# Batch 0 of a gated attention and mixer kernel: 64-row mode and mirror blocks from its third block on, and one spaced list of loads

## The chip, the core and the metric

The kernel runs on one core of a Trainium2 chip. The metric is the device time of one execution in microseconds (us), as the median of several runs. The span of a profile is a little shorter than that time, since it begins with the first instruction and ends with the last.

TensorE multiplies matrices into PSUM[...]. ScalarE (ACT) and VectorE (DVE) read PSUM and write SBUF. GpSimd (POOL) and SyncE (SP) here mainly start DMA transfers: GpSimd the loads from HBM, which turn float32 into bfloat16 on the way, SyncE the transposes from SBUF to SBUF and the stores.

## What is computed

For each of 8 batches, with S = 3008 rows and D = 256 columns (z has 64 columns):

```python
scores = (z @ z.T) / S
attn = maximum(scores, 0) ** 2
x = u * (attn @ v)                          # gated attention: the mixer's input
h = maximum(x.T @ w_tok1, 0) @ w_tok2       # token mixer, 3008 -> 256 -> 3008
u2 = x + h.T
out = u2 + maximum(u2 @ w_ch1, 0) @ w_ch2   # channel mixer, 256 -> 1536 -> 256
```

The matrix of scores is symmetric. So is its relu squared: the block of rows g and columns q is the transpose of the block of rows q and columns g.

## The kernel before

**Tiles.** The 3008 columns are cut into six query blocks q of 512 (the last has 448), the rows into six groups g of four tiles of 128. A block (b, q, g) of the attention matrix is made by two *score units* of two tiles each. A unit is two matmuls of 64 rows that run side by side in TensorE's upper and lower half (z has only 64 columns), into a pair of PSUM banks. ScalarE takes the pair out with a relu (line 461), VectorE squares it in place (469), and the result lies in one of six `at` buffers. When all six g have been multiplied with v, block q is finished, gated with u into `xT`, and turned by a DMA transpose into `x_sb`.

**Mirror blocks.** `direct_block` says which blocks are scored. For batches 1 to 7 these are the ones with g >= q; the block below the diagonal is a *flip*: a DMA transpose of the whole `at` buffer (`flip`, line 514) into an `fl` buffer. An `at` buffer that is flipped comes free only when the transpose has read it. On the diagonal only the triangle is scored and its other half turned in place (`flip_tiles`, 507). In batch 0 all 36 blocks are scored and nothing is flipped. The `fl` buffers (ten) first hold batch 0's six slices of v.

**Two modes of TensorE.** *Half*: pairs of 64-row matmuls. Scores are always in this mode, and so are batches 1 to 7's attention times v (line 644): the upper and the lower 64 rows of a tile go to two banks of a pair, and at the end of a block ScalarE copies one of them out (725), VectorE adds the other (729) and gates the sum (749). *Full*: 128-row matmuls. Batch 0's attention times v runs in it (`whole_matmul`, line 561), into one bank for each half of the 256 columns, and is gated straight from there. The mixer is always full. While a block is *whole*, score units are issued in runs of up to three, to change the mode less often. Two PSUM banks are whole blocks' accumulators; when the last whole block is done they become a fourth pair for the ring of pairs that all else shares (`ring`, `take_slot`).

**The planner.** The order of instructions is decided when the kernel is built, by a loop (from line 1199) that keeps a clock of its own for TensorE, ScalarE, VectorE and SyncE with costs written in the code. At each step it picks a score unit, a piece of attention times v ("av"), or a piece of the mixer. The pieces of a batch's mixer are added when its last block ends: `tok1` (line 800), `tok2` (h_ps, 818), `ch1` (hp, 862), `ch2` (op, 906). A budget spreads them over the next batch. On the chip only semaphores hold: each engine runs its list in order and waits for what it needs.

**Loads.** Before, batch 0's loads are bound to positions in the order of attention blocks (`at_group`): z and v of batch 1, u, and then the four weights (`items`). They carry no wait but for their buffers. From batch 1 on, loads are asked for by `ask`, and `ask_some` lets one go at least `SPACING` = 4.5 us of the planner's clock after the one before. Ahead of it GpSimd copies one element of the newest squared block (`after`, line 120), so that on the chip the load starts no earlier than that.

```python
if asks and pe[0] >= last_ask[0] + SPACING and asks[0][1]():
    last_ask[0] = pe[0]
    if recent[0] is not None:
        after(recent[0])
    asks.pop(0)[0]()
```

Of the kernel before, what the change touches and what calls it, by code (L numbers as in the profile page):

```python
# [55 lines left out]
def kernel(  # L56
# [141 lines left out]
    def load_v(b, c):  # L198
        if b == 0:

            vt = sb.tile([P, GK, D], BF16, tag="fl", name="v_sb", bufs=ROOM["fl"])
            live["fl"] += 1
        else:
            vt = sb.tile([P, GK, D], BF16, tag="v", name="v_sb", bufs=8)
        n = full_tiles[c]
        nc.gpsimd.dma_start(out=vt[:, :n, :], in_=rows_of(v[b], c))
        if n < GK:
            for r in range(2):
                nc.gpsimd.dma_start(
                    out=vt[r * TAIL:(r + 1) * TAIL, n, :], in_=last_rows(v[b]))  # L210
        vs[b, c] = vt
        v_in[b, c] = Done(pe[0] + 9.0 if b > 1 else 0.0)
        loading(LOAD)

    def load_u(b, q):
# [47 lines left out]

    zTs, vs, urs, uTs, xTs, xs = {}, {}, {}, {}, {}, {}
    v_in = {}
    attn = {}

    def direct_block(b, q, g):  # L270

        return b == 0 or g >= q

    def flips(b, q, g):

# [255 lines left out]
    class Block:  # L531
        def __init__(self, b, q):
            self.b, self.q, self.W = b, q, widths[q]
            self.todo = key_order(b, q)[1]
            self.slot = 0
            self.g = None
            self.steps, self.half = [], 0
            self.acc = [None] * DT
            self.home = [None] * DT
            self.begun = set()  # L540
            self.whole = b == 0
            self.tails = False
            self.parts = {}

# [57 lines left out]
    def do_whole(start, g):  # L602
        blk = cur[0]
        begins = blk.g is None
        if begins:
            blk.g, blk.half = g, 0
            blk.todo.remove(g)
            blk.slot += 1
            blk.parts.setdefault(g, 2 if g == LAST else 1)
            n = grain(blk.b, blk.q, g)  # L610
            tiles = list(range(GK - 1 if g == LAST else GK))
            blk.steps = [(dh, tiles[i:i + n]) for i in range(0, GK, n) for dh in range(DT)]
        final = blk.slot == NG
        if begins:
            if final and not blk.tails:
                do_tails(blk, max(start, tails_ready(blk)))
                start = pe[0]
        dh, tiles = blk.steps[blk.half]
        start, end = on_pe(start, "full", len(tiles) * column_time(blk.W))
        for i in tiles:  # L620
            whole_matmul(blk, g, i, dh, final and i == tiles[-1])
        if final:
            acc_free[dh] = push(
                "dve", end + 0.21, 0.61, 0.75,
                lambda t, dh=dh: gate(blk, dh, blk.acc[dh], t), first=1,
                room=("xT", "x") if dh == 0 else lambda: (blk.b, blk.q) in xTs)
        blk.half += 1
        if blk.half == len(blk.steps):
            blk.g = None
            finished(blk, g)  # L630
            if final:
                end_block(blk)
                if blk.q == NQ - 1:
                    ring.append((acc_free[-1], RING))

    def av_matmul(blk, g, i, dh, h, stop):
# [39 lines left out]
    def do_half(start, g):  # L676
# [25 lines left out]
        if blk.half == len(blk.steps):  # L702
            blk.g = None
            _, _, name, uses = blocks.pop((blk.b, blk.q, g))
            release(name, uses, pe[0] + 0.2)
            used[blk.b, g] = used.get((blk.b, g), 0) + 1
            if final:
                end_block(blk)

# [6 lines left out]
    def finish(blk, dh, end):  # L716


        W, acc = blk.W, blk.acc[dh]
        summed = Done()  # L720
        ring.append((summed, blk.home[dh]))

        def copy(t):
            cp = sb.tile([P, QW], F32, tag="res", name="cp", bufs=3)
            nc.scalar.copy(cp[:, :W], acc[:, 1, :W])  # L725
            push("dve", t, 0.66, 0.78, lambda t: add(cp, t), first=1, done=summed)

        def add(cp, t):
            nc.vector.tensor_add(cp[:, :W], acc[:, 0, :W], cp[:, :W])  # L729
            push("dve", t, 0.58, 0.7, lambda t: gate(blk, dh, cp, t), first=1,  # L730
                 room=(lambda: (blk.b, blk.q) in uTs and has_room(("xT", "x"))) if dh == 0
                 else lambda: (blk.b, blk.q) in xTs)

        push("act", end + 0.21, 0.46, 0.61, copy, first=1)

    gated = [0]

    def gate(blk, dh, acc, t):
        b, q, W = blk.b, blk.q, blk.W
        uT = uTs[b, q]  # L740
        if dh == 0:
            xTs[b, q] = sb.tile([P, DT, QW], BF16, tag="xT", name="xT", bufs=ROOM["xT"])
            live["xT"] += 1
            live["x"] += 1
            if W < QW:
                nc.gpsimd.memset(xTs[b, q][:, :, W:], 0.0)
        xT = xTs[b, q]
# [8 lines left out]
        if dh == DT - 1:  # L756
            gated[0] += 1
            push("sp", t, 1.25, 7.5, lambda t: turn_x(b, q, t), first=1)

    def turn_x(b, q, t):  # L760
        x = sb.tile([P, DT, QW // P, P], BF16, tag="x", name="x_sb", bufs=ROOM["x"])
        nc.sync.dma_start_transpose(
            out=x.rearrange("p h t d -> p (h t) d"),
            in_=xTs[b, q].rearrange("p h s -> p (h s)"))
# [18 lines left out]
    def add_mixer(b):  # L783
# [6 lines left out]
        def tok1(q, end):  # L790
# [2 lines left out]
                st["a_ps"] = bank_pair(st["a_slot"], "a_ps")[:, 0, :].rearrange(  # L793
                    "p (h d) -> p h d", h=DT)
            x = xs.pop((b, q))
            live["x"] -= 1
            for i in range(QW // P):
                k = q * (QW // P) + i
                for th in range(2):
# [147 lines left out]
            heads.append(Piece(0.874, [x_done[b, NQ - 1]], lambda end, q=q: tok1(q, end),  # L947
                               opens=q < NQ - 1, closes=q > 0))
        for q in range(NQ):
            heads.append(Piece(4 * column_time(widths[q]), [a_done],  # L950
                               lambda end, q=q: tok2(q, end)))
        def add_ch1(q, c2):
            h2_done[q, c2] = Done()
# [113 lines left out]
    def ask(fn, ready=None):  # L1067
        asks.append((fn, ready or (lambda: True)))

    def ask_some():  # L1070


        while later and later[0][1]() and pe[0] >= later[0][0]:
            later.pop(0)[2]()
        if asks and pe[0] >= last_ask[0] + SPACING and asks[0][1]():
            last_ask[0] = pe[0]
            if recent[0] is not None:
                after(recent[0])
            asks.pop(0)[0]()

    def u_then_turn(m):
        load_u(m // NQ, m % NQ)
# [8 lines left out]
    for b in range(B):  # L1091
        base = b * NQ * NG
        for q in range(NQ):
            m = b * NQ + q + 2
            if m < B * NQ:
                if b == 0:
                    at_group(base + q * NG + 2, lambda m=m: load_u(m // NQ, m % NQ))
                    at_group(base + q * NG + 5, lambda m=m: turn_u(m // NQ, m % NQ))
                else:
# [1 line left out]
        if b + 1 < B:  # L1101
            at_group(base + NG, lambda b=b: new_zT(b + 1))
            for j, c in enumerate(vorder):
                if b == 0:
                    at_group(base + NG + j, lambda b=b, j=j: load_z(b + 1, j))
                    if j % 3 == 2:
                        at_group(base + NG + j // 3 + 8, lambda b=b, j=j: turn_next_z(b, j // 3))
                else:
                    at_group(base + 2 * NG + 2 + j,
                             lambda b=b, j=j: ask(lambda: z_then_turn(b + 1, j)))  # L1110
                    at_group(base + (NQ - 1) * NG - 2 + (j if j > 1 else 0),
                             lambda b=b, c=c, j=j: ask(
                                 lambda: load_v(b + 1, c),
                                 lambda: j < 2 or used.get((b, vorder[j - 2]), 0) == NQ))
    def late_z(c, landed):


# [36 lines left out]

    at_group(6, lambda: turn_u(0, 1))
    w_done = [Done() for _ in range(4)]

    def ask_w_ch(part):
        load_w_ch(part)
        w_done[part].t = pe[0] + 16.0  # L1160


    items = [lambda c=c: load_v(1, c) for c in vorder]
    items += [lambda c=c: load_w_tok1(c) for c in range(NG)]
    items += [lambda c=c: load_w_tok2(c) for c in range(NG)]
    items += [lambda part=part: ask_w_ch(part) for part in range(4)]
    for k, item in enumerate(items):
        at_group(NG + 1 + k * (NQ * NG - 2 * NG + 4) // len(items), item)

    per_batch = 0.87 * NQ * (2 + CHT // 2) + 1.35 * 4 * NQ  # L1170
    flat = NQ * NG * 1.73 + NQ * (NQ + 1) / 2 * 0.44
# [21 lines left out]
    STARVED = 0.7  # L1193
    BACKLOG = 0.9
    SWING = 2.0
    SPACING = 4.5
    SLOW = 0.84
    LONG = 12.0
    while cur[0] is not None or heads or tails:
        run_engines(pe[0])  # L1200
        ask_some()
# [33 lines left out]
        queued = max(free["act"], t) + sum(op.busy for op in waiting["act"]) - t  # L1235


        spare = True
        if blk is not None and not runs:
            if None in blk.acc:  # L1240
                spare = len(slots) > 1 and slots[1] <= t + NOW
            elif blk.slot == NG and blk.g is None:
                spare = len(slots) > 1
            elif blk.slot == NG and blk.half == len(blk.steps) - 1:
                spare = len(slots) > 1 and slots[1] <= t + 0.8

        between = blk is None or blk.acc[0] is None
        mixer_now = tm <= t + NOW and (budget > -SWING or blk is None)
        pick = None

        together = (
# [2 lines left out]
        if not runs:  # L1254
            if mode[0] == "full" and mixer_now:
                pick = "mixer"
            elif mode[0] == "half" and between and budget > LONG and mixer_now:
                pick = "mixer"
            elif n_now and spare and queued < BACKLOG and ts <= t + NOW:
                pick = "scores"  # L1260
            elif ta <= t + NOW:
                pick = "av"
            elif n_now and spare and ts <= t + NOW:
                pick = "scores"
            elif mixer_now:
                pick = "mixer"
# [12 lines left out]
            pick = "av"  # L1279
        if pick is None:  # L1280
            options = [(ta, "av"), (tm, "mixer")]
            if n_now and (whole or low if runs else spare):
                options.append((ts, "scores"))
            when, what = min(options)
            op = next_op()
# [58 lines left out]
```

## Time and profile before

| what | before |
|---|---|
| time, median of 3 | 1154.92 us (1154.44 to 1154.99) |
| span of the profiled execution | 1152.1 us |
| score matmuls (64 rows) | 732 |
| attention times v, 128 rows / 64 rows | 288 / 3948 |
| flips of whole blocks, median from issue to landing | 105, 4.9 us |
| last attention matmul of batch 0, about | 91 us |

Engines' busy times are sums of what the profiler shows. A matmul's shown duration contains its way through the array, so neighbours overlap: a row of "mean 376 ns" can start every 216 ns. "64*128" is a matmul on half of the rows. In the chain and the waits, "A <- B" says that A waited for B. For a DMA, "issue" is the time on the queue that starts it and "landing" is when its last byte is in place.

### The profile page before, as it was taken

The page shows a single profiled execution, that of the slowest core. Times are in us where ns is not written, and L with a number is a line of the kernel's source. Part 1 is how long each engine was busy: PE and PEld are TensorE (multiplying, and loading weights), DVE is VectorE, ACT ScalarE, POOL GpSimd, SP SyncE. Part 2 cuts the span into 40 slices and gives each one's busy share as a digit, 9 for nine tenths or more (in the row PEclk, how much of TensorE's full clock was granted, in tenths as well). Part 3 has the DMA queues.
Part 4 walks back from the last instruction along what each step waited for, and adds up shares of the span by engine and source line. Part 5 has one row for each costly group of instructions (what it writes and reads, how often), then busy time and mean ns, then how long its engine had stood idle before and what let it go on. Part 6 is the DMA issues. An engine that isn't in the chain of part 4 may idle for free.

```text
span 1152.1 us, 22026 instructions
## 1 busy us (share of the span) xinstructions
PE 1141.6 (99%) x8989; PEld 652.5 (57%) x8989; DVE 627.6 (54%) x940; ACT 552.0 (48%) x706; POOL 148.4 (13%) x387
## 2 busy tenths in 40 slices
PE   9999999999999999999999999999999999999998
PEld 3335464655556465575565655656556555566666
DVE  6666754456535664447545475453655556433544
ACT  7887633355434733437435364253463555422321
POOL 4500001110112001210011100121012110000000
PEclk9999999999999999999999999999999999999999
DMA  9998957899869959799488985789759997632121
GB/s 162 182 184 147 182 132 131 142 176 161 150 130 184 162 126 164 130 193 170 105 156 141 188 169 116 147 136 185 149 111 182 158 181 157 129 87 56 51 83 64
DMA packets 472517, 165.80 MB, mean 144 GB/s; under 512 B 436257, under 2 KB 450145, under 8 KB 472417
## 3 DMA queue, kind: packets, MB, share of 16 engines
q1 hardware_dynamic: 444560, 131.70, 56.5%
q0 software_dynamic: 27344, 32.32, 21.1%
q8 instruction: 70, 1.15, 0.4%
q10 hardware_dynamic: 512, 0.38, 0.1%
q14 instruction: 31, 0.25, 0.1%
HBM read 65.40 MB, written 24.64 MB: 78 GB/s over the span
## 4 chain that ended last, share of the span: by engine, by line
PE 95%; DMA 2%; ACT 1%; DVE 1%; SPq 0%; issue 0%; POOL 0%; ACTq 0%; DVEq 0%
PE acc L644 35%; PE op L906 21%; PE hp L862 21%; PE sc L423 6%; PE first_acc L561 5%; PE h_ps L818 3%; PE a_ps L800 3%; DMA fl<-at 1%; ACT at L461 1%; DMA zf<-in_z_dram 1%; DMA at<-at 0%; DMA v_sb<-in_v_dram 0%; SPq L510 0%; DVE h2pre L878 0%; DVE xT L749 0%
## 5 line engine op out<-in xcount | busy, mean ns | idle before, releaser
L461 ACT ACTIVATE at<-sc 128x1024 bf16<-128x1024 f32 (+1 forms) x284 | 279.6, 1021 | 96.3 <-PE sc L423 88.1
L644 PEld LDWEIGHTS <-v_sb 64*128 64x128 bf16 x3948 | 201.3, 94 | 211.1 <-issue 7.2
L876 ACT ACTIVATE h2pre<-hp 128x1024 bf16<-128x1024 f32 (+1 forms) x163 | 163.2, 1003 | 296.4 <-PE hp L862 296.3
L644 PE MATMUL acc<-at,v_sb 64*128 64x512 bf16 x2268 | 280.3, 375 | 0.2 <-DMA at<-at 0.2
L469 DVE TENSOR_TENSOR at<-at 128x1024 bf16<-128x1024 bf16 (+1 forms) x284 | 195.0, 689 | 141.1 <-ACT at L461 139.1
L862 PE MATMUL hp<-xT,w_ch_sb 128*128 128x512 bf16 (+1 forms) x1152 | 257.4, 375 | 0.0
L906 PE MATMUL op<-w_ch_sb,h2pre 128*128 128x256 bf16 x2208 | 251.4, 273 | 0.3 <-DVE h2pre L878 0.2
L906 PEld LDWEIGHTS <-h2pre 128*128 128x128 bf16 x2208 | 215.2, 98 | 39.0 <-issue 3.3
L878 DVE TENSOR_SCALAR h2pre<-hp 128x1024 bf16<-128x1024 f32 (+1 forms) x125 | 150.9, 1208 | 97.3 <-PE hp L862 96.8
L644 PE MATMUL acc<-fl,v_sb 64*128 64x512 bf16 (+1 forms) x1680 | 193.6, 367 | 0.8 <-DVE xT L827 0.7
L862 PEld LDWEIGHTS <-w_ch_sb 128*128 128x128 bf16 x1152 | 111.6, 98 | 126.1 <-issue 5.7
L919 DVE TENSOR_TENSOR res<-op,u_sb 128x512 f32<-128x512 f32 x87 | 60.2, 692 | 142.8 <-PE op L906 140.8
L423 PE MATMUL sc<-zT 64*128 64x512 bf16 (+1 forms) x732 | 124.5, 358 | 0.6 <-ACT at L461 0.3
L729 DVE TENSOR_TENSOR cp<-acc,cp 128x512 f32<-128x512 f32 (+1 forms) x84 | 56.3, 675 | 91.3 <-ACT cp L725 90.5
L725 ACT COPY cp<-acc 128x512 f32<-128x512 f32 (+1 forms) x84 | 48.7, 580 | 102.8 <-PE acc L644 102.5
L449 ACT ACTIVATE at<-sc 128x512 bf16<-128x512 f32 (+3 forms) x164 | 60.8, 438 | 39.9 <-PE sc L423 38.1
L561 PE MATMUL first_acc<-at,v_sb 128*128 128x512 bf16 (+2 forms) x288 | 65.6, 376 | 1.3 <-DMA v_sb<-in_v_dram 1.3
L423 PEld LDWEIGHTS <-zT 64*128 64x128 bf16 x732 | 37.7, 94 | 46.8 <-issue 12.6
L498 DVE TENSOR_TENSOR at<-at 128x512 bf16<-128x512 bf16 (+3 forms) x164 | 45.5, 322 | 25.4 <-ACT at L449 24.3
L827 DVE TENSOR_TENSOR xT<-xT,h_ps 128x1024 bf16<-128x1024 bf16 (+1 forms) x48 | 55.2, 1173 | 7.1 <-PE h_ps L818 6.8
L749 DVE TENSOR_TENSOR xT<-cp,uT 128x512 bf16<-128x512 f32 (+1 forms) x84 | 55.4, 665 | 0.8
L120 POOL CAST mark<-at 128x1 f32<-128x1 bf16 x48 | 10.2, 213 | 334.2 <-DVE at L469 334.2
(55 smaller groups left out, 369.0 us busy)
## 6 DMA issues: line engine op xcount, KB each, us to landing
out_dram<-res SPq DMA_DIRECT2D x87, 256.0 KB, 2.3
v_sb<-in_v_dram POOLq DMA_DIRECT2D x40, 256.0 KB, 5.7
ur<-in_u_dram POOLq DMA_DIRECT2D x40, 256.0 KB, 5.5
w_tok_sb<-in_moe_w_tok_dram POOLq DMA_DIRECT2D x10, 256.0 KB, 9.2
zs<-in_z_dram POOLq DMA_DIRECT2D x35, 64.0 KB, 3.7
at<-at SPq DMA_TRANSPOSE x123, 2.7
fl<-at SPq DMA_TRANSPOSE x105, 4.9
v_sb<-in_v_dram POOLq DMA_DIRECT2D x8, 192.0 KB, 5.7
```

The costliest lines, as they stand in the source:

```text
L423: nc.tensor.matmul(sc[:, r, c0:c1], zT[h, k:k + P], zT[h, m + c0:m + c1], start=True, stop=True)
L449: nc.scalar.activation(a3[:, i, c0:c1], sc[:, r, c0:c1], ACT.Relu, scale=inv_S)
L461: nc.scalar.activation(view, sv, ACT.Relu, scale=inv_S)
L469: nc.vector.tensor_mul(view, view, view)
L561: nc.tensor.matmul(o, vs[blk.b, g][rows, i, dh * P:(dh + 1) * P], rhs, start=first, stop=stop, skip_group_check=True)
L644: nc.tensor.matmul(o, vs[blk.b, g][rows, i, dh * P:(dh + 1) * P], rhs, start=(dh, h) not in blk.begun, stop=stop, skip_group_check=True)
L729: nc.vector.tensor_add(cp[:, :W], acc[:, 0, :W], cp[:, :W])
L862: nc.tensor.matmul(hp[:, r, :W], w_ch1_sb[:, dc, cc * P:(cc + 1) * P], xT[:, dc, :W], start=(dc == 0), stop=(dc == DT - 1))
L876: nc.scalar.activation(h2[:, :, :W], hp[:, :, :W], ACT.Relu)
L878: nc.vector.tensor_single_scalar(h2[:, :, :W], hp[:, :, :W], 0.0, AX.max)
L906: nc.tensor.matmul(op[:, i, :], h2, w_ch2_sb[:, cc, :], start=(cc == 0 and (i == 0 or apart)), stop=(cc == CHT - 1), skip_group_check=True)
L919: nc.vector.tensor_add(res.rearrange("p i (h d) -> p i h d", d=P), op.rearrange("p i (h d) -> p i h d", d=P), us[:, :, half * 2:half * 2 + ...
```

## The change

Batch 0's blocks q = 0 and 1 stay whole. From q = 2 on the batch runs in half mode, and with g >= 2 it uses the symmetry: six blocks, (3,2), (4,2), (4,3), (5,2), (5,3) and (5,4), become flips instead of scores. To leave DMA room for these flips, every load from block 1 on goes through one list, one load per 2.4 us of the planner's clock in batches 0 and 1; the weights are taken from it only when nothing else is due. As they come later, the mixer doesn't begin before batch 1's third block (`OPENING`). The copy at the end of a half block of batch 0 goes to whichever of ScalarE and VectorE is less loaded, and batch 0's `x_sb` uses the buffers of `h2`, which are idle then.

```diff
-        return b == 0 or g >= q
+        return g >= q or (b == 0 and g < MIRROR)          # WHOLE, MIRROR = 2, 2
...
-            self.whole = b == 0
+            self.whole = b == 0 and q < WHOLE
...
-                if blk.q == NQ - 1:
+                if blk.q == WHOLE - 1:
                     ring.append((acc_free[-1], RING))
...
+        on_act = blk.b > 0 or load("act") + 0.46 < load("dve") + 0.67
...
+    def x_home(b):
+        return "x" if b else "h2"
...
-            heads.append(Piece(4 * column_time(widths[q]), [a_done],
+            heads.append(Piece(4 * column_time(widths[q]), [a_done, tok2_done[q]],
...
-        if asks and pe[0] >= last_ask[0] + SPACING and asks[0][1]():
-            last_ask[0] = pe[0]
-            if recent[0] is not None:
-                after(recent[0])
-            asks.pop(0)[0]()
+        spacing = SPACING if cur[0] is None or cur[0].b > 1 else FIRST_SPACING
+        if pe[0] < last_ask[0] + spacing:
+            return
+        if asks and asks[0][1]():
+            fn = asks.pop(0)[0]
+        elif spare:
+            fn = spare.pop(0)
+        else:
+            return
+        last_ask[0] = pe[0]
+        if recent[0] is not None:
+            after(recent[0])
+        fn()
...
-    items = [lambda c=c: load_v(1, c) for c in vorder]
-    items += [lambda c=c: load_w_tok1(c) for c in range(NG)]
-    items += [lambda c=c: load_w_tok2(c) for c in range(NG)]
-    items += [lambda part=part: ask_w_ch(part) for part in range(4)]
-    for k, item in enumerate(items):
-        at_group(NG + 1 + k * (NQ * NG - 2 * NG + 4) // len(items), item)
+    weights = [lambda c=c: load_w_tok1(c) for c in range(NG)]
+    weights += [lambda c=c: ask_w_tok2(c) for c in range(NG)]
+    weights += [lambda part=part: ask_w_ch(part) for part in range(4)]
+    at_group(NG + 1, lambda: spare.extend(weights))
+    for k, c in enumerate(vorder):
+        at_group(3 * NG + k, lambda c=c: ask(lambda: load_v(1, c)))
...
-    SPACING = 4.5
+    FIRST_SPACING, SPACING = 2.4, 4.5
+    OPENING = NQ + 2
...
-        mixer_now = tm <= t + NOW and (budget > -SWING or blk is None)
+        opening = blk is not None and blk.b * NQ + blk.q < OPENING
+        mixer_now = tm <= t + NOW and (budget > -SWING or blk is None) and not opening
```

## The prediction

> **What bounds the kernel now.** I read the page's first part, the list of waits, a piece of the timeline and then the DMA views, because the answer of each raises the next question.
>
> ```profile
> PE 1141.6 (99%) x8989; PEld 652.5 (57%) x8989; DVE 627.6 (54%) x940; ACT 552.0 (48%) x706; POOL 148.4 (13%) x387
> ```
>
> TensorE is bound from end to end. So a gain has to come out of its instruction stream or out of its few holes, which the list of waits for TensorE names:
>
> ```profile
> PE a_ps L800 <- ACT at L461: 0.9, 1, 0.9
> PE h_ps L818 <- ACT at L461: 0.8, 2, 0.6
> PE acc L644 <- DVE xT L827: 0.7, 1, 0.7
> PE acc L644 <- DMA at<-at: 0.2, 1, 0.2
> ```
>
> A busy share overstates a pipelined engine, so I took starts of matmuls in the trace instead. A 128-row matmul of 512 columns starts 216 ns after the one before; two 64-row ones together take 217 ns. The timeline shows what a change between the two modes costs:
>
> ```profile
> 61.90 0.82 PE L423 MATMUL sc<-zT 64*128 64x512 bf16 x6
> 62.65 2.76 PE L561 MATMUL first_acc<-at,v_sb 128*128 128x512 bf16 x12
> 65.34 0.61 PE L423 MATMUL sc<-zT 64*128 64x512 bf16 x4
> ```
>
> From 62.65 to 65.34 is 2.69 us for twelve matmuls of 0.216, 2.59: 0.10 is the switch. With 0.095 a switch, the 8989 matmuls need 1125.5 + 114 x 0.095 = 1136.3 us. The first starts at 1.2, the last ends at 1147.7: 10.1 us are holes. By the starts, 3.8 of them lie before 20 us, 0.6 at 102 (the scores waiting for ScalarE), 2.4 between 122 and 131 (around the h_ps burst), 1.1 at 238, and the rest in crumbs.
>
> The second reading is the DMA, by stretches (last two numbers: busy share of its engines, GB/s):
>
> ```profile
> 50.00:75.00 25.00, 25.00 (x134) 9.71 (x133) 17.86 (x27) 21.27 (x23) 5.38 (x9) 1.00 1.25 189
> 100.00:125.00 25.00, 24.07 (x213) 12.92 (x208) 14.15 (x26) 17.18 (x24) 0.92 (x3) 1.00 1.06 187
> ```
>
> It is full while TensorE notices nothing, because in batch 0 nothing that TensorE needs soon comes from a transpose. From 36 to 75 us the loads take most of it:
>
> ```profile
> q0 software_dynamic: 4036, 5.35, 81.1%
> q1 hardware_dynamic: 7910, 1.94, 40.3%
> ```
>
> The zT transposes behind them took a median of 16.1 us from issue to landing. The view of the flips from 88 to 125 us, where one load at a time is under way, says:
>
> ```profile
> L517 SPq DMA_TRANSPOSE fl<-at x9: 1582/1949/5817, 90.9 to 122.2; - x9
>   ACT at L461: 1.9, 2
> DMA to landing us min/median/max: 3.9/5.8/7.9
> ```
>
> A flip holds SyncE for 1.95 us and lands 3.9 to 7.9 us after its issue; ScalarE has already waited 1.9 us for a buffer that a flip was still reading.
>
> **What the skill says.** "TensorEngine Tiling (Array Packing)", Key Properties: changing the tiling mode drains TensorE. The trace agrees, 0.10 us each. "DMA: Bandwidth & Descriptors", Issuing engines are not separate DMA queues: transfers of all engines run on the same 16 DMA engines and interleave. The trace agrees (zT 16.1 us beside loads; 2.5 to 2.8 us alone later on). The same page, Latency and other measured facts, gives 261 GB/s for DMA transposes; a flip moves 0.524 MB, so an estimate is 2.0 us, beside 1.95 measured on SyncE.
>
> **The change part by part.**
>
> *64-row mode from block (0,2) on.* The streaming time of attention times values stays (288 x 0.216 against pairs of 0.217). What goes is switching: in whole mode every run of three score units costs two. In the order of the changed program I count 86 switches for 114: 28 x 0.095 = 2.7 us off the path, as TensorE has nothing else then. It adds, for 4 blocks x 2 halves, a copy (0.48 on ScalarE or 0.60 on VectorE back to back) and an add (0.60). ScalarE: 12 units x 0.92 + 2 x 0.48 = 12.0 us in a block of 13.0 us of TensorE; hidden, barely. VectorE: 12 x 0.61 + 6 x 0.60 = 10.9; hidden.
>
> *Six mirror blocks.* (3,2), (4,2), (4,3), (5,2), (5,3), (5,4) are no longer scored: 12 units x 0.216 (four of them 0.19) and, in the counts, 732 score matmuls become 708: 72.1 to 69.7 us, so 2.4 us off. ScalarE loses 12 x 0.92, VectorE 12 x 0.61, both slack. In their place come six flips: 6 x 1.95 us of SyncE and of DMA, at 34 to 66 us.
>
> The stream is then 1123.0 + 8.2 = 1131.2 us: **5.1 us less**, if holes stay.
>
> *Spaced list, weights last.* Before, loads of batch 0 carried no wait and ran ahead. Now each follows a marker on GpSimd that waits for the newest squared block, one per about 2.9 us of TensorE's work. Behind the marker only later loads are queued; the weights, at the end, are wanted only by the mixer, which begins later. A load costs the DMA about 1.28 us (39 us x 81.1/121.4 over 20.4 loads of 0.262 MB). So DMA is 44% taken by loads, and the flips live on the rest.
>
> *Does the flips' queue keep up?* This is the unknown cost. SyncE's queue is in order. From 34 us (TensorE's work time, holes left out) to the flip of block (0,3,5), fl_798, stand four flips, two x, one u and five z transposes: 4 x 1.95 + 3 x 1.26 + 5 x 1.2 = 17.6 us, with seven loads of 1.28 between, 9.0: it is served at 60.6 and lands 2 us later, 62.6. Who wants it: block (0,4,1) was given the buffer that this flip still reads (buffers of the changed program); its score is issued at 58.2, and the PSUM bank of that score is the next acc1's at 60.2. ScalarE must begin by 59.2: 3.4 us late. With 1.0 us a load it is 1.5, with transposes at the 2.9 us of the 88-125 stretch (81% of 37 us over 5.5 MB) it is over 7. I take 2.5, as loads of one at a time leave gaps.
> Between 77 and 105 us there are 17.5 us of transposes (five flips for batch 1) and 7 loads, 9.0: the triangle of (1,1), at_1263, lands near 105.5 and is wanted at 104.6, with the first 2.5 us already giving it time: 1.0. fl_1560 at 114 and at_1447 at 129 have margins near zero: 0.5. Sum **4.0 us of new holes**, ends 0.5 and 15.
>
> *Mixer from block 8.* The pieces are the same (2256 + 1152 + 192 + 384 matmuls in both orders) and only come later. The holes of 102 and 122-131, 3.0 us, go with the old order; but the new one has five h_ps in a row with only two free PSUM pairs, each evacuated in 1.13 us by VectorE against 0.86 of TensorE: 5 x 0.27 = 1.35, plus the bank's turn-round of 0.2 twice: 1.8 back. x of batch 0 moving into h2's buffers, and the tok2 waits, cost nothing: no h2 is alive before the first ch1 at 126 us, and the last tok2 slice is asked for 15 us ahead of its use.
>
> Total: -5.1 + 4.0 - 3.0 + 1.8 = -2.3, rounded to the profile's crumbs: 1154.9 - 2.6 = **1152.3 us**.
>
> **Rivals.**
> A, *the queue falls behind*: with transposes slowed by loads as at 36-75 us, holes come to 8 to 15 us (fl_798 5 to 8, at_1263 and fl_1247 3 to 4, at_1447 2 to 3). Then 1154.9 - 5.1 - 3.0 + 1.8 + 10 = 1158.6, slower. For it: DMA at 187-189 GB/s already, 3.1 MB more flips in the same stretch, the 16.1 us of zT. Against: there the loads ran ahead in a heap; now they are spaced.
> B, *it cancels*: holes of 6 us give 1154.6.
> C, *all hidden*: the queue keeps up as after 250 us, where TensorE has crumbs only, and the h_ps burst costs nothing: 1154.9 - 5.1 - 3.0 = 1146.8 or, with the usual crumb, 1147.5.
>
> **How the numbers follow.** My forecast (holes 2 to 5): 0.35; C: 0.15; B: 0.2; A: 0.3. Faster by over 0.2% (below 1152.6) is C and most of my forecast, 0.5; same 0.2; slower 0.3. Range 1147.3 to 1160.0: C's end is in, and of A the far half is out.
>
> **What would show it.** Right: the switches' 2.7 us and the scores' 2.4 us in TensorE's starts before 110 us; a wait of ScalarE for fl<-at of 1 to 4 us near 64 us (60 + 3.9 of start holes); flips landing 4 to 15 us after their issue. Wrong: TensorE holes over 8 us between 50 and 135 us, by fl<-at or at<-at; or TensorE waiting for ScalarE in every block, which would mean that 12.0 of 13.0 us is too tight; or weights landing after tok1 (near 108 us).

## The result, and the profile after

The changed kernel takes 1171.53 us (median of 4 runs, 1170.83 to 1173.65); the kernel before took 1154.95 beside it. The ratio is 1.0147, 95% interval 1.0130 to 1.0165: 17 us slower. The forecast was 1152.3. On the chips of the experiments further down, some runs of most kernels took about 10 us longer than the rest (17 of 55 runs of the kernel before on one chip), which makes the intervals wide; a ratio leaves out runs over 1.5% above the fastest of their kernel.

First the busy row, TensorE's row in the 40 slices and the clock granted to it, from the page of the changed kernel:

```profile
PE 1143.4 (98%) x9149; PEld 662.5 (57%) x9149; DVE 625.8 (54%) x938; ACT 546.3 (47%) x700; POOL 155.2 (13%) x419
...
PE   9987899999999999999999999999999999999998
...
PEclk9998999999999999999999999999999999999999
```

TensorE's busy share hardly moved. The slices show where to look: the third to fifth (58 to 146 us). Next, TensorE's waits in the changed kernel (us in total, times, longest):

```profile
PE sc L424 <- ACT at L462: 6.2, 2, 5.9
PE acc L645 <- ACT at L462: 5.7, 1, 5.7
PE acc L645 <- DMA at<-at: 4.2, 2, 2.3
```

Two waits for ScalarE of nearly 6 us and two for the triangle (the diagonal block whose other half is turned in place) are new. ScalarE's own waits between 40 and 170 us say what it waited for:

```profile
ACT at L462 <- DMA fl<-at: 15.1, 4, 6.6
```

A flip still reads the buffer into which ScalarE is to write: the chain is TensorE, ScalarE, flip. The flips around the first long hole, between 57 and 70 us:

```profile
L518 SPq DMA_TRANSPOSE fl<-at x2: 2937/3110/3282, 61.6 to 65.0; - x2
...
  ACT at L462: 6.3, 1
...
DMA to landing us min/median/max: 5.0/5.9/6.7
```

The one that ScalarE waits for was issued at 61.6 us and landed 6.7 us later, at 68.3. The flips between 88 and 125 us, in the view that the prediction showed of before:

```profile
L518 SPq DMA_TRANSPOSE fl<-at x5: 3882/4677/6576, 87.8 to 112.3; - x5
...
  ACT at L462: 8.8, 3
...
DMA to landing us min/median/max: 7.3/9.5/12.3
```

The median flip held SyncE 1.95 us before and 4.7 now; it landed 5.8 us after its issue before and 9.5 now. The table of stretches, two of the kernel before and then the changed kernel's (TensorE's busy time comes second, the last three numbers are granted clock, DMA share and GB/s):

```profile
125.00:150.00 25.00, 23.98 (x173) 12.20 (x171) 19.74 (x30) 14.06 (x20) 3.23 (x8) 1.00 0.95 178
150.00:175.00 25.00, 25.00 (x185) 17.65 (x184) 10.99 (x12) 6.14 (x6) 1.42 (x4) 1.00 0.48 116
```

```profile
50.00:75.00 25.00, 18.79 (x162) 9.19 (x160) 14.41 (x23) 14.01 (x16) 6.06 (x14) 0.93 1.02 179
75.00:100.00 25.00, 25.00 (x248) 13.20 (x245) 19.25 (x35) 20.38 (x26) 8.07 (x21) 1.00 1.11 179
100.00:125.00 25.00, 18.76 (x148) 8.93 (x146) 9.03 (x16) 9.50 (x14) 6.93 (x16) 0.86 1.22 178
125.00:150.00 25.00, 20.79 (x158) 10.45 (x155) 8.74 (x12) 7.69 (x9) 4.68 (x12) 0.93 1.19 191
150.00:175.00 25.00, 23.01 (x163) 10.26 (x162) 17.52 (x28) 16.04 (x23) 4.71 (x12) 1.00 1.17 187
```

Two things are to be seen. The DMA's share is over 1 from 50 to 175 us; before, it was 0.95 at 125 to 150 and 0.48 at 150 to 175. That alone stops nothing: at 50 to 75 us the share is lower than before (1.02, before 1.25), and only now does somebody wait there for a flip. And the clock is no longer 1.00: a mean of 0.86 in 25 us is 7 us at half clock, 0.93 is 3.5. TensorE's timeline shows how the two hang together:

```profile
61.94 1.91 PE L645 MATMUL acc<-at,v_sb 64*128 64x512 bf16 x16
69.50 1.89 PE L645 MATMUL acc<-at,v_sb 64*128 64x512 bf16 x8 [5.65 <-ACT at L462]
...
103.89 1.04 PE L645 MATMUL acc<-at,v_sb 64*128 64x512 bf16 x8
110.80 0.61 PE L424 MATMUL sc<-zT 64*128 64x512 bf16 x2 [5.86 <-ACT at L462]
111.18 1.93 PE L645 MATMUL acc<-at,v_sb 64*128 64x512 bf16 x8
```

Eight matmuls take 1.04 us at 103.89 and 1.9 just after the two standstills. The clock records say 0.5 for 3.41 us from 68.8, for 6.83 us from 109.7 and for 3.41 us from 130.2.

The sum, by starts of matmuls against the streaming time of the instructions (the time that they need one right behind the other): the stream fell by 5.1 us, as forecast. What comes on top of it rose from 10.1 to 32.4: 17.7 are waits for flips and triangles (6.6 up to 70 us, 6.6 around 105, 4.5 at 125 to 130), 5.8 is work at half clock (1.3, 2.8 and 1.7 after these), 2.8 lies around the h_ps burst, 6.1 is all the rest. -5.1 + 22.3 = 17.2; the span grew by 17.4.

### The profile page after: what moved, and what is told of

It reads as the page before. It is cut to its first block, busy times and chain, and to the rows that moved or that the text cites. A ratio compares the mean times of both kernels' runs of the same rounds, so it can differ in the third digit from the quotient of the medians.

```text
span 1169.5 us, 22413 instructions
## 1 busy us (share of the span) xinstructions
PE 1143.4 (98%) x9149; PEld 662.5 (57%) x9149; DVE 625.8 (54%) x938; ACT 546.3 (47%) x700; POOL 155.2 (13%) x419
## 4 chain that ended last, share of the span: by engine, by line
PE 92%; DMA 4%; ACT 1%; DVE 1%; SPq 0%; issue 0%; ACTq 0%; DVEq 0%
PE acc L645 36%; PE op L923 21%; PE hp L879 21%; PE sc L424 5%; PE a_ps L817 4%; PE h_ps L835 3%; DMA fl<-at 3%; PE first_acc L562 2%; DMA at<-at 1%; ACT at L462 1%; DVE xT L844 0%; DMA out_dram<-res 0%; SPq L228 0%; DVE h2pre L895 0%; PE wp L195 0%
## 5 line engine op out<-in xcount | busy, mean ns | idle before, releaser
L645 PEld LDWEIGHTS <-v_sb 64*128 64x128 bf16 x4324 | 226.9, 94 | 239.4 <-issue 24.4
L645 PE MATMUL acc<-at,v_sb 64*128 64x512 bf16 (+1 forms) x2548 | 317.5, 377 | 9.9 <-ACT at L462 5.7
L462 ACT ACTIVATE at<-sc 128x1024 bf16<-128x1024 f32 (+1 forms) x272 | 270.5, 1022 | 84.4 <-PE sc L424 61.0
L470 DVE TENSOR_TENSOR at<-at 128x1024 bf16<-128x1024 bf16 (+1 forms) x272 | 186.9, 690 | 140.4 <-ACT at L462 137.8
L645 PE MATMUL acc<-fl,v_sb 64*128 64x512 bf16 (+1 forms) x1776 | 208.3, 369 | 0.6 <-DMA fl<-at 0.6
L424 PE MATMUL sc<-zT 64*128 64x512 bf16 (+1 forms) x708 | 126.9, 360 | 6.8 <-ACT at L462 6.2
L740 DVE TENSOR_TENSOR cp<-acc,cp 128x512 f32<-128x512 f32 (+1 forms) x92 | 61.7, 675 | 107.5 <-ACT cp L734 106.8
L120 POOL CAST mark<-at 128x1 f32<-128x1 bf16 x90 | 20.5, 228 | 404.1 <-DVE at L470 403.8
L761 DVE TENSOR_TENSOR xT<-cp,uT 128x512 bf16<-128x512 f32 (+1 forms) x92 | 60.4, 664 | 1.1
L835 PE MATMUL h_ps<-w_tok_sb,a_sb 128*128 128x512 bf16 (+1 forms) x192 | 48.3, 375 | 0.9 <-DVE xT L844 0.6
```

Of the source, the lines that this page charges most:

```text
L424: nc.tensor.matmul(sc[:, r, c0:c1], zT[h, k:k + P], zT[h, m + c0:m + c1], start=True, stop=True)
L462: nc.scalar.activation(view, sv, ACT.Relu, scale=inv_S)
L470: nc.vector.tensor_mul(view, view, view)
L645: nc.tensor.matmul(o, vs[blk.b, g][rows, i, dh * P:(dh + 1) * P], rhs, start=(dh, h) not in blk.begun, stop=stop, skip_group_check=True)
L761: nc.vector.tensor_mul(xT[:, dh, :full * P].rearrange("p (t s) -> p t s", s=P), acc[:, :full * P].rearrange("p (t s) -> p t s", s=P), uT[: ...
L835: nc.tensor.matmul(h[:, dh, :W], st["a"][:, th, dh * P:(dh + 1) * P], w_tok2_sb[:, th, q * QW:q * QW + W], start=(th == 0), stop=(th == 1))
```

## The experiments

Theory Q: the mirror flips and the loads together overfill what moves data between 35 and 160 us; flips land late, ScalarE and then TensorE stand still. "Ratio" is to the kernel before on the same chip; "profiled" is the time of the run whose profile is read.

| run | median (lowest to highest) us | profiled us | ratio, 95% interval |
|---|---|---|---|
| e1_no_mirror | 1164.57 (1162.85 to 1188.42) | 1180.80 | 1.0042, 1.0011 to 1.0072 |
| e2_list_only | 1163.79 (1158.61 to 1168.04) | 1158.61 | 1.0042, 1.0014 to 1.0070 |
| e3_open_first | 1169.33 (1168.96 to 1170.02) | 1168.96 | 1.0110, 1.0079 to 1.0140 |
| e4_at7 | 1184.46 (1177.98 to 1199.19) | 1199.19 | 1.0221, 1.0172 to 1.0270 |
| e5_no_weights | 1158.06 (1154.50 to 1162.64) | 1162.64 | 1.0003, 0.9962 to 1.0045 |
| e6_kept_busy | 1178.73 (1174.09 to 1188.73) | 1188.73 | 1.0210, 1.0158 to 1.0262 |
| e7_half_only | 1155.94 (1154.94 to 1174.50) | 1165.85 | 0.9990, 0.9949 to 1.0030 |
| e8_old_list | 1182.17 (1178.72 to 1183.97) | 1178.72 | 1.0225, 1.0206 to 1.0243 |
| e9_flips_added | 1171.55 (1166.03 to 1183.11) | 1176.16 | 1.0120, 1.0032 to 1.0208 |
| e10_half_kept_busy | 1155.32 (1153.94 to 1167.39) | 1154.03 | 1.0000, 0.9970 to 1.0029 |
| e11_u_later | 1158.99 (1152.95 to 1171.01) | 1171.01 | 1.0009, 0.9977 to 1.0041 |
| e12_half_opening | 1158.53 (1154.12 to 1172.37) | 1172.37 | 0.9998, 0.9965 to 1.0030 |
| e13_loads_added | 1175.86 (1168.43 to 1186.92) | 1168.43 | 1.0135, 1.0042 to 1.0228 |
| e15_spacing | 1187.37 (1187.12 to 1190.90) | 1187.27 | 1.0265, 1.0195 to 1.0336 |
| e16_changed_again | 1172.78 (1171.82 to 1178.05) | 1178.05 | 1.0139, 1.0078 to 1.0200 |

### Which part of the change costs

Without the mirror blocks:

```diff
-    WHOLE, MIRROR = 2, 2
+    WHOLE, MIRROR = 2, 6
```

> Batch 0 keeps 64-row mode from its third block, but scores all 36 blocks: no flips in batch 0, 12 more score units, stream 1133.4 us against 1131.2 of the changed kernel. Theory Q (the DMA queue of flips falls behind): the hole of 5.9 us near 64 us and the half clock after it (1.7 us) go, the later ones at 105 and 125 us shrink since the queue starts them less late; 1155 to 1163 us. Rival H (64-row mode itself overloads ScalarE and VectorE in batch 0): holes stay in batch 0's half blocks, and with 12 more units they grow; 1171 us or more.

1.0042 for 1.0147: the six mirrors, which take 2.4 us off the stream, cost 7 us by the medians of this run and of the changed kernel, and 12 by the ratios. Rival H falls: the 64-row mode with 12 units more is faster, not slower.

The list and the later mixer alone:

```diff
-    WHOLE, MIRROR = 2, 2
+    WHOLE, MIRROR = 6, 6
```

> Batch 0 all whole as before the change, with the new list of loads and the mixer from batch 1's third block; stream 1125.5 + 124 x 0.095 = 1137.2 us, 0.9 above the kernel before. Theory Q: no hole before 95 us; at 100 to 135 us the flips of batch 1's first two blocks still meet the weights' loads with no mixer between, holes of 5 to 10 us; 1158 to 1166 us. Rival H: all harm comes with 64-row mode, so this one is at 1155 to 1157 us.

Slower than before with the same arithmetic. Its timeline has no hole of 1 us or more between 20 and 100 us and then

```profile
101.54 1.03 PE L645 MATMUL acc<-at,v_sb 64*128 64x512 bf16 x8
105.63 0.61 PE L424 MATMUL sc<-zT 64*128 64x512 bf16 x2 [3.07 <-ACT at L462]
106.01 1.94 PE L645 MATMUL acc<-at,v_sb 64*128 64x512 bf16 x8
```

one wait of 3.1 us and half clock after it. The loads that the list moved back now stand beside batch 1's flips; that these are the reason, and not the later mixer, is not separated here (e12 below has the later mixer without the list and shows no such cost).

The list taken out, the mirrors kept (the asking loop of before comes back with it):

```diff
-    at_group(NG + 1, lambda: spare.extend(weights))
-    for k, c in enumerate(vorder):
-        at_group(3 * NG + k, lambda c=c: ask(lambda: load_v(1, c)))
+    items = [lambda c=c: load_v(1, c) for c in vorder] + weights
+    for k, item in enumerate(items):
+        at_group(NG + 1 + k * (NQ * NG - 2 * NG + 4) // len(items), item)
```

> The changed kernel with the old places of all loads (none waits for a marker, weights at their old blocks, all in by 86 us): 64-row mode, six mirror blocks and the opening of the mixer stay. Theory Q: the flips now meet loads in a heap, so the hole near 63 us grows to 6 to 12 us with a half-clock stretch after it, while between 90 and 135 us, where the weights are gone, holes fall to under 6: 1156 to 1168 us. Rival S (the spaced list is what costs, the flips get through anyway): no hole over 2 us before 80 us, 1148 to 1153.

Direction right, size not: 1182. In its profile the three long holes are 9.0, 12.7 and 5.6 us, all between 51 and 91 us; from 100 to 150 us they sum to 0.2. So with mirrors the spaced list gains 9 us (by the ratios), and without them (e2) it costs. Rival S of this run falls.

The 64-row mode alone, with the loads of before:

```diff
-    WHOLE, MIRROR = 2, 2
+    WHOLE, MIRROR = 2, 6
...
-    OPENING = NQ + 2
+    OPENING = 0
```

> The kernel before with the 64-row mode from block (0,2) on and nothing else of the change: no mirror blocks, the old places of all loads, the mixer free to begin as before. Its stream counts 70 switches and all 732 score matmuls: 1132.1 us for 1136.3 of before. Theory Q (only transposes that something waits for suffer from the loads, and this kernel has none in batch 0): no new holes before 90 us, 1149.5 to 1152.5 us. Rival T (the 64-row mode itself costs, as ScalarE with 12.0 us of work in 13.0 us of a block is too tight): holes of 1 us or more in each of the four blocks, 1154 or more.

No gain, though the stream is 4.2 us shorter. Where it went is read from e10 below, the same kernel with twelve matmuls more: at three block ends TensorE waits for ScalarE, by the starts 1.4, 1.3 and 1.1 us in all. The first two:

```profile
65.05 0.82 PE L439 MATMUL sc<-zT 64*128 64x512 bf16 x4
66.55 0.39 PE L439 MATMUL sc<-zT 64*128 64x512 bf16 x2 [0.69 <-ACT at L477]
...
78.91 0.56 PE L439 MATMUL sc<-zT 64*128 64x448 bf16 x4
80.28 0.36 PE L439 MATMUL sc<-zT 64*128 64x448 bf16 x2 [0.82 <-ACT at L477]
```

That is rival T's mechanism at three of four blocks, 3.8 us of the 4.2. In batch 0 of the changed kernel, with 12 units less for ScalarE, these waits are absent.

The mixer from batch 1's first block on:

```diff
-    OPENING = NQ + 2
+    OPENING = NQ
```

> The changed kernel with the mixer allowed from batch 1's first block. Theory Q: the hole near 64 us stays (5.9 us); mixer pieces stand between the flips of batch 1, so the holes at 105 and 125 us shrink by half or more, and the half clock with them; 1158 to 1165 us. Rival M (the late mixer is all of the harm): 1157 us or less. Rival H: 1170 us or more.

Better by 2 us (medians) to 4 (ratios); all three expectations missed. The hole near 64 us stands ahead of any mixer (a wait of 5.7 us again), and the later ones only moved: 3.7 us from 110 and 3.6 from 137.

A seventh buffer for squared blocks, taken from the flips':

```diff
-    ROOM = {"at": 6, "fl": 10, ...}
+    ROOM = {"at": 7, "fl": 9, ...}
```

> The changed kernel with 7 buffers for at instead of 6 (and 9 for fl instead of 10, to make room). Theory Q: the queue has more to do than it can, and one buffer more only lets ScalarE run some 2 us further ahead; holes shrink by 2 us once or twice: 1165 to 1171 us. Rival B (too few buffers, the queue is fast enough): the holes at 64 and 105 us go, 1157 us or less.

Slower by 7 us (lowest run) to 13 (median) instead of faster; Q's range is missed too. ScalarE's waits for flips are still there, 40.1 us of them in this profile; why they grew is open, since the order of the instructions changed too.

### Loads or transposes

The sixteen weight loads left out:

```diff
-        nc.gpsimd.dma_start(
-            out=w_tok2_sb[:, :, cols],
-            in_=moe_w_tok2.rearrange("(tc t) s -> t tc s", t=P)[:, :, cols])
+        nc.gpsimd.memset(w_tok2_sb[:, :, cols], 0.01)
```

(and the same for the other three weights)

> The changed kernel with its sixteen weight loads left out: GpSimd writes a constant into each weight tile where the load stood, so the mixer multiplies by constants. TensorE's stream is that of the changed kernel. Theory Q (flips and triangles land late because loads share the DMA engines with them, and each long hole adds a half-clock stretch): only two weight loads stand ahead of the hole at 63 us, so most of that one stays (4 to 6 us), while the 16 us of holes between 100 and 130 us, where the loads of the weights' second half stand between the flips, fall below 6: 1150 to 1160 us. Rival L (the flips of the new 64-row blocks and of batch 1 are too many for the transposes by themselves, loads or none): the holes after 100 us stay over 12 us, 1166 or more.

As Q said, with one hole elsewhere than thought: the loss is no longer seen, to within 0.4%. Waits and stretches of this run:

```profile
PE acc L635 <- ACT at L452: 8.4, 2, 5.1
```

```profile
75.00:100.00 25.00, 19.85 (x174) 10.25 (x170) 13.72 (x22) 15.20 (x17) 5.61 (x12) 0.86 0.90 89
100.00:125.00 25.00, 24.81 (x231) 12.89 (x228) 14.71 (x31) 14.83 (x23) 11.66 (x22) 1.00 1.08 184
```

Between 100 and 125 us TensorE is whole again with the same flips; two holes, at 64 and 81 us, remain. Rival L falls.

Is it SyncE's queue that is full, or the DMA engines? Twelve transposes that nobody reads, added to the kernel before:

```diff
+    extra = []
+
+    def extra_flip(n):
+        if n < 4:
+            extra.append(sb.tile([P, 2, GK * DT, P], BF16, tag="fl", name="extra", bufs=ROOM["fl"]))
+        for h in range(2):
+            nc.sync.dma_start_transpose(
+                out=extra[n % 4][:, h], in_=vs[0, n % 2].rearrange("p t d -> p (t d)"))
+        on_sp(2.5)
+
+    for n, group in enumerate([13, 20, 21, 22, 23, 25]):
+        at_group(group, lambda n=n: extra_flip(n))
```

> The kernel before with twelve transposes of half a flip's size added on SyncE where the changed kernel has its six mirror flips (planned at 37, 53, 55, 57, 59 and 64 us), from values already in SBUF into a buffer that nobody reads. Nothing in TensorE's stream changes and no score waits for them. Theory Q (SyncE's queue and the DMA engines are full in that stretch, so twelve more transposes delay the gates, the first scores of batch 1 and its flips, whoever reads them): new holes of 3 to 12 us between 50 and 135 us, 1158 to 1168. Rival D (only the dependency hurts, scores waiting for buffers that a flip still reads; transposes that nobody waits for are hidden): 1154 to 1157.

and the same bytes as loads, past SyncE:

```diff
-            nc.sync.dma_start_transpose(
-                out=extra[n % 4][:, h], in_=vs[0, n % 2].rearrange("p t d -> p (t d)"))
+            nc.gpsimd.dma_start(
+                out=extra[n % 4][:, h].rearrange("p (t h) d -> p t (h d)", t=GK),
+                in_=rows_of(v[0], h))
-        on_sp(2.5)
```

> The kernel before with twelve more loads of 0.262 MB, issued by GpSimd where the run with added flips has its twelve transposes, into the same buffers that nobody reads. The bytes are those of the added flips; SyncE's queue gets nothing. Theory E (the DMA engines are what is full): the same loss as with the added transposes, holes of 8 us or more between 75 and 125 us, 1164 to 1176. Rival S (SyncE's queue in order is what is full: a transpose holds it until it has been handed on): the loads slide into the idle time of the engines, 1155 to 1159.

No run of either is under 1166, where the lowest of before beside them are 1154.3 and 1154.1. First TensorE's longest wait with the transposes, then with the loads:

```profile
PE first_acc L561 <- DVE xT L749: 9.4, 1, 9.4
```

```profile
PE first_acc L561 <- DVE xT L749: 10.5, 1, 10.5
```

The same wait at the same place: the gate of batch 0's fifth block has no u yet. The way there differs. The view of uT between 60 and 110 us, first with the added transposes, then with the added loads:

```profile
L228 SPq DMA_TRANSPOSE uT<-ur x3: 1253/1608/2614, 83.1 to 109.9; - x3
...
DMA to landing us min/median/max: 3.8/4.7/5.4
```

```profile
L228 SPq DMA_TRANSPOSE uT<-ur x4: 1259/3187/4195, 71.0 to 94.6; - x4
...
  DMA uT<-ur: 11.1, 1
...
DMA to landing us min/median/max: 5.1/8.6/17.7
```

The kernel before issued that transpose at 67.9 us, and it landed after 5.7. With the added transposes it stood in SyncE's queue until 83.1 and landed 4.7 us later; with the added loads it was issued at 71.0 and took 17.7 to land. So 3.1 MB more in that stretch cost some 12 us (lowest run against lowest: 12 and 14; the intervals reach from 4 to 26), whoever issues them and though nothing waits for them: they delay a transfer that is waited for. Loads alone do it, and with them SyncE's longest hold by a transpose grows too, from 9.0 us (zT at 50.3) to 13.0 (zT at 49.9), with nothing added to its queue. So the DMA engines are what is full. Rivals D and S fall. The Trainium skill, "DMA: Bandwidth & Descriptors", Issuing engines are not separate DMA queues, says that transfers of all issuing engines run on the same 16 DMA engines; the two runs agree (1.0120 and 1.0135). Both runs have the old, crowded places of the loads, so the 12 us are not a price for the spaced list.

The list's pace:

```diff
-    FIRST_SPACING, SPACING = 2.4, 4.5
+    FIRST_SPACING, SPACING = 1.6, 4.5
```

> The changed kernel with loads asked every 1.6 us of the plan instead of 2.4, so that the list ends near 82 us of the plan and not near 117. Theory Q (the DMA's work from 35 to 160 us is the bound, and who asks when only moves the holes): holes move from after 100 us to before it, the time lies between the changed kernel and the one with the old places of the loads: 1170 to 1180. Rival W (it is the weights' standing beside batch 1's flips that costs): the holes after 100 us go and those at 60 us stay, 1158 to 1166.

1187, worse than Q's range. The holes did move ahead: one wait for a flip at 54 us takes 20.1 us, two thirds of what is lost between 50 and 100. Yet those after 100 us did not go (one of 6.0 us at 124), so rival W falls.

The changed kernel again on that chip:

> The changed kernel as it is, on the chip of these two runs: 1168 to 1176 if the result carries over to another chip; the holes near 63, 105 and 125 us at the same places, each but the last with half clock after it, if they come from the order of the transposes and not from chance.

It repeats, 1.0139: in its profile the longest holes are at 67, 113 and 131 us, each with half clock after it, the last too.

### The half clock

Matmuls of zeros ahead of the waiting ones in the changed kernel (the helper adds them to a sum under way, with start=False):

```diff
+        if (blk.b, blk.q, blk.slot, dh) == (0, 4, 1, 1):
+            keep_busy("a", 22, blk.acc[0][:, 0, :])
```

(likewise 22 ahead of the scores near 105 us, and 8 ahead of each of the triangle's matmuls)

> The changed kernel with matmuls of zeros added in front of the matmuls that wait longest (22 before the one of 5.9 us near 63 us, 22 before the one of 5.9 us near 105 us, 8 before each of the first waits for the triangle near 125 us), accumulating zeros into a sum under way, so that nothing is computed otherwise. Theory K (the clock is halved because TensorE stood still): the waits end when they did, but the three stretches at half clock after them (13.6 us, 6.8 us of work lost) shrink or go: 1163 to 1168 us. Rival F (the half clock has another cause, or the added matmuls simply take their time): the stretches stay and the time is that of the changed kernel or more, 1171 to 1180.

By the clock theory K, by the time rival F: the two shortest runs reached a mean clock of 0.999 and 1.000, where the changed kernel's had 0.992 to 0.996, but took 1174.1 and 1176.1 us. A cleaner trial, in the kernel with the 64-row mode alone, whose one long hole near 130 us is the last:

```diff
+            if (at_work.b, at_work.q, at_work.slot, at_work.g) == (1, 1, NG - 1, None):
+                keep_busy("hole", 12, at_work.acc[0][:, 0, :])
```

> The 64-row mode alone, as in the run of that, with twelve matmuls of zeros (2.6 us and two switches) in front of the one scores matmul that stood still for 3.3 us near 130 us, accumulating zeros into a sum under way. Behind it no transposes are late any more. Theory K (the clock is halved because TensorE stood still, and what the half clock loses there is not made up): the wait ends when it did, the 3.4 us at half clock vanish, 1.7 us less: 1153.2 to 1154.4 where the version without has 1155.4. Rival F (half clock with another cause): 3.4 us at half clock stay and the time is 1155.2 to 1156.5.

The hole comes from the same wait in both profiles, but at another time, since e7's has a stand of 10 us at 81 us that e10's has not. In e7 ScalarE waits 4.4 us for a flip until 132.8, in e10 4.1 us until 121.4, and the added matmuls run from 119.6 to 122.4. So the stretch with the hole is 125 to 150 us without the added matmuls (e7) and 100 to 125 us with them (e10):

```profile
125.00:150.00 25.00, 21.94 (x174) 9.95 (x172) 15.97 (x26) 13.45 (x20) 1.98 (x5) 0.93 1.08 190
```

```profile
100.00:125.00 25.00, 24.91 (x217) 13.74 (x213) 12.91 (x25) 15.79 (x24) 0.72 (x2) 1.00 1.03 180
```

The clock stays whole. Other runs say the same: of those under 1160 us, five of e7's seven have a mean clock of 0.998, and all fourteen of e10's have 0.999 or 1.000. That the standstill halves the clock is shown; that 1.7 us come back is not: e10's median, 1155.32, lies in rival F's range, and the ratios of e7 and e10, 0.9990 and 1.0000, can't be told apart.

### Towards a better version

Both start from e7:

```diff
-                    at_group(base + q * NG + 2, lambda m=m: ask(lambda: u_then_turn(m)))
+                    at_group(base + q * NG + (5 if b == 1 else 2),
+                             lambda m=m: ask(lambda: u_then_turn(m)))
```

> The 64-row mode alone, with the u loads that batch 1's blocks ask for asked three score groups later, so that the load which met a flip at 125 us (5.1 us on SyncE instead of 1.95) meets another stretch. Theory Q: the hole of 3.3 us near 130 and its half clock go, 1150 to 1153 us, if the load does not now delay the triangle's transposes at 112 to 116 us of the plan. Rival P (the flip would have been late without the load): 1155 to 1157.

```diff
-    OPENING = 0
+    OPENING = NQ + 2
```

> The 64-row mode with the later opening of the mixer (from batch 1's third block), the old places of the loads, no mirror blocks. Stream 1132.5 us. Theory Q: with no mixer between them the first two blocks of batch 1 want their eight flips and triangle at TensorE's pace of 13 us a block, which the queue can't keep beside the loads of u: holes of 4 us or more between 95 and 125 us, 1155 to 1160. Rival M (the old order of the mixer makes the holes at 102 and 122 to 131 us): those go, 1149 to 1152.

Neither can be told from the kernel before; the lowest run, 1152.95, is 0.1% under its lowest. No version here beats it measurably.

## Why the prediction was wrong

- **The stream, -5.1 us.** Right: with 708 score matmuls and 86 switches, stream and holes account for the span's change to 0.2 us.
- **Copies and adds hidden beside 64-row blocks.** Right in the changed kernel. Without the mirrors it fails at three block ends, which e10 shows.
- **Old holes gone, h_ps burst 1.8 us.** Near enough: the burst is 2.8 (149 to 158 us), other holes are 6.1 where 7.1 were left in the sum. The total of -2.3 then became -2.6 by "crumbs" for which no working is given; the sum as it stands is 1152.6.
- **"Does the flips' queue keep up?", 4.0 us.** The step that failed. fl_798 was priced at 2.5 and cost 5.8; at_1263 at 1.0 and cost 4.5; the scores at 105 us, behind fl_1247, were priced at nothing and cost 6.0, and two crumbs before these (at 51 and 100 us) 1.3. The text had the waiting chain, the victims (rival A named fl_1247) and both ends. What it had wrong is how long a flip is under way. The order of the queue came as counted: three flips, two x, one u and five z transposes stand ahead of the flip that ends ScalarE's wait, and SyncE let go of that one at 64.9 us, some 60.3 of TensorE's work time, where the text has 60.6. But "lands 2 us later" is SyncE's hold of 1.95 us taken for the transfer; from issue to landing it took 6.7 us, and the flip behind the hole at 105 us took 12.3. The view in the prediction already had 3.9 to 7.9. "I take 2.5, as loads of one at a time leave gaps" went further down, when its own ledger gave 3.4. The 261 GB/s behind the estimate of 2.0 us stand, on the page of the Trainium skill that the prediction names there, for transposes with a middle dimension that is not contiguous; here the first of these flips moved its 0.524 MB at 78 GB/s.
- **Why the transfers take so long.** A ledger of one queue asks when one flip is served. What it leaves out is that transfers under way together stretch each other: in every stretch from 50 to 175 us the changed kernel moves 178 to 191 GB/s, and e9 and e13 show that 3.1 MB more there delay even a transfer that has nothing to do with them. Why the rate stays near 180 is open; in the kernel before, short pieces of the stretch from 100 to 125 us, where loads are few, reach 290.
- **"The weights, at the end, are wanted only by the mixer."** True and beside the point: nobody waits for them, but they share the engines with batch 1's flips. Without their bytes the loss is no longer seen (e5).
- **The clock.** Not in the sum at all: 5.8 us. The Trainium skill, "TensorE: Matmul & The Clock Gate", What's actually happening, has a half rate after an idle window of about 3.4 us; the trace shows the 0.5 and the pieces of 3.41 us.
- **What would show it.** "TensorE holes over 8 us between 50 and 135 us, by fl<-at or at<-at" is what came: 17.7.

Rival A (1158.6, chance 0.3) had the direction and the cause. With its 15 us of holes at the far end and the clock's 5.8 it would have been 1169. Still open: how much of the 5.8 us the next wait for DMA would have taken anyway (e6 got the clock back and not the time).

## What to carry to other kernels

Where the DMA's share is at 1 and TensorE notices nothing, an added transfer has to be set against the sum of the stretch, not only against its own reader: here 3.1 MB cost some 12 us, by either issuing engine. A transfer's price there is its time from issue to landing as measured in that stretch, not the time that it holds its queue. A recomputation that is replaced by a transfer (2.4 us of TensorE for 3.1 MB) belongs only where the DMA has room. And a hole of some 3 us can be dearer than it looks, since the first 3 to 6 us of work after it can run at half clock.

## What the runs showed of the hardware

The half clock comes in pieces of 3.41 us, and within a run all pieces lie on one grid: in the changed kernel they begin at 68.79, 109.75 and 130.23 us, 12 and 6 pieces apart. In e15, TensorE stood from 54 to 74 us and the half clock lasted from 59.0 to 79.5: the halving starts during a long stand, and its price is what follows the end, 1.3 to 2.8 us a hole in the changed kernel.

What decides is how long TensorE stood within one piece of the grid (time without streaming, by starts of matmuls, from 20 to 1145 us in all 17 kept traces). Half clock began after every piece with 2.2 us or more of standing and after none with less than 2.06; between these, e6 has 2.07 with it and e12 2.08 without. It ended after every piece with 0.78 us or less and after none with 0.87 or more. So where a stand falls counts as much as its length. e2's stand of 3.2 us, 2.8 of it in one piece, brought the half clock; in the changed kernel two waits of 2.5 and 2.1 us at 125 us, 2.8 in one piece, did so too; in e11 a stand of 3.1 us at 398 us, split into 1.4 and 1.8, did not. The Trainium skill's page on the clock gate, in the section named above, has an idle window of about 3.4 us; by these traces 2.1 to 2.2 us of standing in such a window were enough.
